# A table of decays in 32 rows with zeros below it, earlier products of zeros, and a second queue for the second batch's inputs

## Chip, cores, metric

One core of a Trainium2 chip (trn2). The metric is the device time of one execution in microseconds (us), as the median of several executions. A profile is one of these executions, recorded.

## The reference

```python
# recurrent attention: batch 4, heads 8, sequence 768, head size 64
for t in range(S):
    state = gamma * state + einsum('bhd,bhe->bhde', k[:, :, t], v[:, :, t])
    y[:, :, t] = scale * einsum('bhd,bhde->bhe', q[:, :, t], state)
# then, on x = y as (3072 tokens, 512):
h = x @ w_in                       # 512 -> 2048
out = maximum(0.01 * h, h) @ w_out # 2048 -> 512
```

## The kernel before

The attention is worked in chunks of 128 tokens. For each chunk and batch, `ap` is the product of k and q, `am` is `ap` under a mask, `yp` is the product of v (already multiplied by its decays) and `am`, and `x` is `yp` times the decays of q, the input of the two big products that fill nearly all of the time. The weights come as 64-bit numbers in pieces (`raw`), which ScalarE (ACT) and VectorE (DVE) turn into 32-bit ones (`w`); the first big product is called `d`.

The opening of the program is all that the change touches:

```python
rows = t[0:H, 1:3]...[:, 0 : decay.shape[1]]          # 8 rows of 780 numbers
nc.scalar.dma_start(out=rows, in_=decay)              # ScalarE's queue
load_qk(0, 0); load_v(0, 0)                           # SyncE's queue, in this order
load_qk(0, 1); load_v(0, 1)
load_piece(0); load_piece(1)
load_qk(0, 2); load_v(0, 2)
# ... [cut: further loads; memset of the mask by VectorE, its triangle by GpSimd]
nothing = t[:, 0, 0, :].bitcast(BF16)
nc.vector.memset(t[:, 0, 0, :], 0.0)                  # 256 columns of zeros
# keep_busy(n): n products of zeros, 512 columns each, into a spare bank
keep_busy(7)
score(0, 0)                                           # ap of batch 0
nc.tensor.matmul(tables[:, 0, 0:H], lhsT=by_head, rhs=ones, ...)          # decays of k
nc.tensor.matmul(tables[:, 0, H : H + HP], lhsT=place, rhs=g_c, ...)
masked(0, 0)                                          # am of batch 0, VectorE
nc.vector.tensor_copy(out=dec[:, n_gq:], in_=tables[:, 0, 0 : H + HP])
nc.tensor.matmul(spread..., lhsT=place, rhs=g_q, ...) # decays of q, 512 columns
nc.scalar.copy(out=dec[:, 0:n_gq], in_=spread...)
decay_v(0, 0, nc.vector)                              # v of batch 0 times its decays
score(0, 1); values(0, 0); masked(0, 1)               # values = yp
decay_v(0, 1)                                         # on GpSimd
keep_busy(1)
# ... [cut] taken(0, 0), values(0, 1), taken(0, 1): x of batches 0 and 1
score(0, 2)
keep_busy(3)
steps = direct(0, 0, x, parts[0][1], 0)               # d
# ... [cut]
```

Of the kernel before, what the change touches and what calls it, by code (L numbers as in the profile page):

```python
# [13 lines left out]
BF16 = mybir.dt.bfloat16  # L14
# [9 lines left out]
def kernel(  # L24
# [35 lines left out]
    nc = tc.nc  # L60
    NC = S // C
    DM = H * D
    HP = H // 2
# [11 lines left out]
    dec = const.tile([128, HP * C + H + HP], FP32, name="dec")  # L75
# [39 lines left out]
    heads = {}  # L115
# [11 lines left out]
            y = flat[:, half : 2 * half].rearrange("p (s h d) -> p s h d", s=2, h=H)  # L127
        heads[c, b] = x, y

    def load_qk(c, b):  # L130
        nc.sync.dma_start(out=heads[c, b][0], in_=qk[c, b])

    def load_v(c, b):
        nc.sync.dma_start(out=heads[c, b][1][:, 1], in_=kv[c, b][:, 1])

    def load_k(c, b):
        nc.sync.dma_start(out=heads[c, b][1][:, 0], in_=kv[c, b][:, 0])
# [1 line left out]
    def load(c, b, place=None):  # L139
        place_for(c, b, place)  # L140
        load_qk(c, b)
        nc.sync.dma_start(out=heads[c, b][1], in_=kv[c, b])

    def decay_v(c, b, engine=nc.gpsimd):
        v = heads[c, b][1][:, 1]
        if engine is not nc.scalar:
            engine.tensor_tensor(out=v, in0=v, in1=gk.unsqueeze(2).to_broadcast([128, H, D]),
                                 op=ALU.mult)
        else:
            for h in range(H):  # L150
                engine.activation(v[:, h], v[:, h], AF.Identity, scale=gk[:, h : h + 1])
# [6 lines left out]
    def score(c, b):  # L158

        x = heads[c, b][0]  # L160
        ps = scores[c, b] = two_banks(f"ap_{c}_{b}")
        for a in range(HP):
            for u in range(2):
                for j in range(2):
                    nc.tensor.matmul(ps[ts(u, 64), j, a, :], lhsT=x[ts(j, 64), 1, a, ts(u, 64)],  # L165
                                     rhs=x[ts(j, 64), 0, a, :])

    def masked(c, b):
        am = work.tile([128, 2, HP, C], FP32, tag="am", bufs=2, name=f"am_{c}_{b}")
        nc.vector.tensor_tensor(  # L170
            out=am.rearrange("p j a t -> p (j a) t"),
            in0=scores[c, b].rearrange("p j a t -> p (j a) t"),
            in1=mask.unsqueeze(1).to_broadcast([128, H, C]), op=ALU.mult)
        scores[c, b] = am
# [102 lines left out]
    def load_piece(n, place=None):  # L277
        if n >= N_PIECES:
            return
        if not f64:  # L280
            nc.sync.dma_start(out=piece(n), in_=weights[n].rearrange("p (h n) -> p h n", h=2))
            return
        if place is None:
            tag, bufs = ("raw", 3) if n < N_PIECES - 4 else (("qk", "kv")[n % 2], AHEAD)
            raws[n] = work.tile([128, W], I64, tag=tag, bufs=bufs, name=f"raw{n}")
        else:
            raws[n] = place.bitcast(I64)
        nc.sync.dma_start(out=raws[n], in_=weights[n])
# [299 lines left out]
    words = tile_x("words").rearrange("p i k n -> p (i k n)")[:, 0 : 2 * W]  # L588
    xs = {0: new_x(0)}
    x, t = xs[0]  # L590
    rows = t[0:H, 1:3].rearrange("p i k n -> p (i k n)")[:, 0 : decay.shape[1]]
    nc.scalar.dma_start(out=rows, in_=decay)
    load_qk(0, 0)
    load_v(0, 0)
    load_qk(0, 1)
    load_v(0, 1)
    load_piece(0)
    load_piece(1)
    load_qk(0, 2)
    load_v(0, 2)  # L600
    load_piece(2)
    load_piece(3, words)
# [14 lines left out]



    nothing = t[:, 0, 0, :].bitcast(BF16)  # L620
    nc.vector.memset(t[:, 0, 0, :], 0.0)
    idle = psum.tile([128, 2, N], FP32, tag="ff", bufs=4, name="idle")

    def keep_busy(n):
        for _ in range(n):
            nc.tensor.matmul(idle.rearrange("p i n -> p (i n)"), lhsT=nothing[:, 0:128],  # L626
                             rhs=nothing, start=True, stop=True, skip_group_check=True)



    tables = psum.tile([128, 2, N], FP32, tag="ff", bufs=4, name="tables")
    spread = psum.tile([128, 2, N], FP32, tag="ff", bufs=4, name="spread")
    n_gq = HP * C
    ends = [0, C, C + H, 2 * C + H, 2 * C + H + n_gq, 2 * C + H + n_gq + HP]
    by_head, ones, place, g_q, g_c = (rows[:, i:j] for i, j in zip(ends, ends[1:]))
    keep_busy(7)
    score(0, 0)
    nc.tensor.matmul(tables[:, 0, 0:H], lhsT=by_head, rhs=ones, start=True, stop=True,
                     skip_group_check=True)
    nc.tensor.matmul(tables[:, 0, H : H + HP], lhsT=place, rhs=g_c, start=False, stop=True,  # L640
                     skip_group_check=True)
    masked(0, 0)
    nc.vector.tensor_copy(out=dec[:, n_gq:], in_=tables[:, 0, 0 : H + HP])
    nc.tensor.matmul(spread.rearrange("p i n -> p (i n)"), lhsT=place, rhs=g_q, start=True,
                     stop=True, skip_group_check=True)
    nc.scalar.copy(out=dec[:, 0:n_gq], in_=spread.rearrange("p i n -> p (i n)"))
    decay_v(0, 0, nc.vector)
    score(0, 1)
    values(0, 0)
    masked(0, 1)  # L650
    decay_v(0, 1)
    keep_busy(1)
    next_powers()
    taken(0, 0, x)
    values(0, 1)
    next_mantissas(lambda: taken(0, 1, x))
    next_powers()
    score(0, 2)
    keep_busy(3)
    steps = direct(0, 0, x, parts[0][1], 0)  # L660
    next(steps)
# [121 lines left out]
def _decay(H, D):  # L783



    import numpy as np

    lg = np.log1p(-(2.0 ** (-5.0 - np.arange(H))))
    t = np.arange(1, C + 1)  # L790
    gq = np.exp(lg[:, None] * t[None, :]) / math.sqrt(D)
    gq = gq.reshape(H // 4, 2, 2, C).transpose(1, 2, 0, 3).reshape(2, -1)
    gc = np.exp(C * lg).reshape(H // 2, 2).T
    place = np.concatenate([np.repeat(np.eye(2), 64, axis=1), gq, gc], axis=1)
    place = np.concatenate([place, np.zeros((H - 2, place.shape[1]))])
    return np.concatenate([np.exp(-lg[:, None] * t[None, :]), np.eye(H), place],
                          axis=1).astype(np.float32)


def _layout(q, k, v, w_in, w_out):  # L800
# [60 lines left out]
```

## Time and profile before

| | before |
|---|---|
| median | 666.92 us of 3 runs (666.7 to 667.69); 666.81 of 6 with those beside the changed kernel |
| span of the profile | 664.9 us, of which TensorE busy 659.4 |
| first q and k land | 4.59 us |
| first `d` | 13.93 us |

The prediction below shows the views that it was read from. The columns used most: the chain of waits has start, length and what; the timeline has start, length, engine, line, operation, operands and, in brackets, the idle time before it and who ended it. The stretches: columns are the stretch, its length, busy time of PE, PEld (TensorE's loading of its left operand), DVE, ACT and POOL with the number of instructions, granted clock (the share of its full clock that TensorE was allowed), mean busy share of the 16 DMA engines, and GB/s. One caution: the trace's record of the clock begins when the full clock is first granted, and what lies before it is shown as 1.00, though the products there run at half rate. Before:

```profile
2.40:3.40 1.00, 1.00 (x4) 0.30 (x2) 0.00 (x0) 0.29 (x1) 0.00 (x0) 1.00 0.89 360
4.00:4.70 0.70, 0.63 (x6) 0.07 (x6) 0.00 (x0) 0.00 (x0) 0.00 (x0) 1.00 0.38 111
```

The DMA engines are busy and fast in the first stretch, and busy for a share of only 0.38 in the second.

### The profile page before, as it was taken

The numbers are of one execution on the slowest core, as the hardware profiler recorded it, in microseconds if no ns is written. First come the engines' busy times: TensorE is split into PE (matmuls) and PEld (weight loads), VectorE is DVE, ScalarE is ACT, GpSimd is POOL, SyncE is SP. The second block draws the span as 40 slices with busy tenths as digits, with TensorE's granted clock in tenths as the row PEclk, the third lists the DMA queues.
The fourth block names the chain that finished last, engine by engine and source line by source line (L and its number), as shares of the span: only waits on it lengthen the run. The fifth ranks groups of instructions, "written<-read, shape, count | busy, mean of one in ns | idle before, by whom it ended". The sixth has DMA issues, their size and how long they took to land.

```text
span 664.9 us, 10405 instructions
## 1 busy us (share of the span) xinstructions
PE 659.4 (99%) x4505; PEld 573.6 (86%) x4505; DVE 373.9 (56%) x570; ACT 175.8 (26%) x322; POOL 20.1 (3%) x22
## 2 busy tenths in 40 slices
PE   8999999999999999999999999999999999999998
PEld 5888888888888888888888888888888888888886
DVE  5789969889888676325543613663431444431342
ACT  5854555264261002212201311210221220221210
POOL 0000000000000111001000100100100000000000
PEclk9999999999999999999999999999999999999999
DMA  8920312313222453003012100301300001000001
GB/s 327 403 97 33 126 64 79 112 65 113 109 85 75 166 184 127 1 1 128 1 46 81 64 1 1 127 1 64 128 1 0 2 0 45 19 1 1 0 1 63
DMA packets 15758, 48.92 MB, mean 74 GB/s; under 512 B 1753, under 2 KB 2009, under 8 KB 15713
## 3 DMA queue, kind: packets, MB, share of 16 engines
q1 hardware_dynamic: 15696, 48.24, 20.1%
q8 instruction: 35, 0.57, 0.3%
q14 instruction: 11, 0.08, 0.0%
q10 hardware_dynamic: 16, 0.02, 0.0%
HBM read 41.97 MB, written 6.29 MB: 73 GB/s over the span
## 4 chain that ended last, share of the span: by engine, by line
PE 99%; DMA 1%; DVE 0%; issue 0%
PE B_o L414 13%; PE A_o L414 13%; PE C_o L414 12%; PE C_h L414 12%; PE B_h L414 12%; PE A_h L414 12%; PE D_o L414 6%; PE D_h L414 6%; PE ap L165 4%; PE yp L193 4%; PE d L436 2%; PE yp L184 2%; PE yp L208 1%; DMA qk<-in_qk_dram 1%; PE sums L208 0%; PE idle L626 0%
## 5 line engine op out<-in xcount | busy, mean ns | idle before, releaser
L414 PE MATMUL A_h<-x,w 128*128 128x256 f32 x368 | 87.0, 379 | 0.0
L414 PEld LDWEIGHTS A_h<-x,w 128*128 128x128 f32 x368 | 69.9, 190 | 9.6 <-issue 0.2
L414 PE MATMUL A_o<-g,w 128*128 128x256 f32 x288 | 68.0, 379 | 0.0
L449 ACT ACTIVATE g<-g 128x512 f32<-128x512 f32 x69 | 42.0, 630 | 92.4 <-DVE g L361 92.4
L414 PEld LDWEIGHTS A_o<-g,w 128*128 128x128 f32 x288 | 54.8, 190 | 7.4
L454 ACT COPY m<-A_h 128x512 f32<-128x512 f32 x23 | 13.4, 582 | 143.6 <-PE A_h L414 103.9
L361 DVE TENSOR_TENSOR m<-m,B_h 128x512 f32<-128x512 f32 x23 | 15.8, 686 | 55.5 <-PE B_h L414 55.5
L361 DVE TENSOR_TENSOR m<-m,B_o 128x512 f32<-128x512 f32 x16 | 11.0, 685 | 63.9 <-PE B_o L414 63.9
L238 DVE TENSOR_TENSOR x<-yp,dec 128x512 f32<-128x512 f32 x24 | 16.4, 689 | 49.7 <-PE yp L208 35.6
L414 PE MATMUL C_h<-t,w 128*128 128x256 f32 x184 | 44.1, 383 | 0.0
L414 PE MATMUL B_h<-x,w 128*128 128x256 f32 x184 | 44.1, 383 | 0.0
L414 PE MATMUL B_h<-t,w 128*128 128x256 f32 x184 | 43.5, 379 | 0.0
L414 PE MATMUL D_h<-t,w 128*128 128x256 f32 x184 | 43.5, 379 | 0.0
L414 PE MATMUL C_h<-x,w 128*128 128x256 f32 x184 | 43.5, 379 | 0.0
L414 PEld LDWEIGHTS C_h<-t,w 128*128 128x128 f32 x184 | 34.5, 190 | 5.5 <-issue 0.9
L414 PEld LDWEIGHTS B_h<-t,w 128*128 128x128 f32 x184 | 35.0, 190 | 4.7
L414 PEld LDWEIGHTS D_h<-t,w 128*128 128x128 f32 x184 | 35.0, 190 | 4.7
L414 PEld LDWEIGHTS C_h<-x,w 128*128 128x128 f32 x184 | 35.0, 190 | 4.7
L414 PEld LDWEIGHTS B_h<-x,w 128*128 128x128 f32 x184 | 34.5, 190 | 5.0 <-issue 0.3
L364 DVE TENSOR_TENSOR gd<-g,gd 128x512 f32<-128x512 f32 x48 | 37.1, 773 | 1.7
L170 DVE TENSOR_TENSOR am<-ap,mask 128x1024 f32<-128x1024 f32 x24 | 28.5, 1220 | 10.8 <-PE ap L165 10.8
L414 PE MATMUL B_o<-gd,w 128*128 128x256 f32 x144 | 34.0, 379 | 0.0
(118 smaller groups left out, 1019.0 us busy)
## 6 DMA issues: line engine op xcount, KB each, us to landing
raw<-in_weights_dram SPq DMA_DIRECT2D x31, 512.0 KB, 4.3
qk<-in_qk_dram SPq DMA_DIRECT2D x19, 512.0 KB, 3.8
kv<-in_kv_dram SPq DMA_DIRECT2D x17, 512.0 KB, 4.4
out_dram<-o SPq DMA_DIRECT2D x23, 256.0 KB, 2.1
in<-in_qk_dram SPq DMA_DIRECT2D x3, 512.0 KB, 8.7
in<-in_kv_dram SPq DMA_DIRECT2D x3, 512.0 KB, 8.5
kv<-in_kv_dram SPq DMA_DIRECT2D x4, 256.0 KB, 7.0
o_in<-in_qk_dram SPq DMA_DIRECT2D x2, 512.0 KB, 8.6
```

The costliest lines, as they stand in the source:

```text
L165: nc.tensor.matmul(ps[ts(u, 64), j, a, :], lhsT=x[ts(j, 64), 1, a, ts(u, 64)], rhs=x[ts(j, 64), 0, a, :])
L170: nc.vector.tensor_tensor(out=am.rearrange("p j a t -> p (j a) t"), in0=scores[c, b].rearrange("p j a t -> p (j a) t"), in1=mask.unsqueeze ...
L184: nc.tensor.matmul(ps[ts(i, 64), j, m, :], lhsT=st[b][ts(j, 64), a, :], rhs=x[ts(j, 64), 0, a, :], start=(m == 0), stop=False, skip_group_ ...
L193: nc.tensor.matmul(ps[ts(i, 64), j, m, :], lhsT=y[:, 1, 2 * a + j, :], rhs=am[:, j, a, :], start=(c == 0 and m == 0), stop=True, skip_grou ...
L208: nc.tensor.matmul(sp[ts(j, 64), a, :], lhsT=y[:, 0, 2 * a + j, :], rhs=y[:, 1, 2 * a + j, :], start=start, stop=True, skip_group_check=True)
L238: nc.vector.tensor_tensor(out=blocks, in0=ps[:, :, 0 : HP // 2, :], in1=gq, op=ALU.mult)
L361: nc.vector.tensor_tensor(out=out, in0=a, in1=b, op=ALU.add)
L364: nc.vector.tensor_tensor(out=out, in0=a, in1=b, op=ALU.subtract)
L414: nc.tensor.matmul(half, lhsT=block(w, sa)[:, k, ts(i, 128)], rhs=rhs[:, k, :], start=(first and (i == 0 or split) and n == 0 and k == 0), ...
L436: nc.tensor.matmul(banks[r][:, i, :], lhsT=block(2 * u, r + 2 * kh)[:, k, ts(i, 128)], rhs=x[:, 2 * kh + th, k, :], start=(step == 0 and i ...
L449: nc.scalar.activation(g[:, i], g[:, i], AF.Prelu, alpha=0.01)
L454: nc.scalar.copy(out=got["m1"], in_=ps)
```

## The change

The intent, as far as it can be read from the code: give the array zeros to multiply sooner and make the table products full ones of 128 rows, so that its clock comes up early; use ScalarE's queue for the second batch's loads so that the hole at 4 us is filled; and take two small jobs from VectorE.

```diff
+    def load_qk(c, b, queue=nc.sync):     # [cut: load_v in the same way]
-    rows = t[0:H, 1:3]...
-    nc.scalar.dma_start(out=rows, in_=decay)
+    rows = t[:, 1:3]...
+    n_rows = decay.shape[0]               # 32: 8 rows and 24 of zeros from memory
+    nc.scalar.dma_start(out=rows[0:n_rows], in_=decay)
+    nc.gpsimd.memset(rows[n_rows:64], 0.0)
+    nc.gpsimd.memset(rows[64:128], 0.0)
+    nothing = t[:, 0, 0, 0:64].bitcast(BF16)
+    nc.vector.memset(t[:, 0, 0, 0:64], 0.0)
-    load_qk(0, 1)
-    load_v(0, 1)
+    load_qk(0, 1, nc.scalar)
+    load_v(0, 1, nc.scalar)
@@ [cut: memset of the mask, now after that of the zeros]
-    keep_busy(7)
+    keep_busy(8)                          # 128 columns read four times over
@@
-    nc.vector.tensor_copy(out=dec[:, n_gq:], in_=tables[:, 0, 0 : H + HP])
+    nc.scalar.copy(out=dec[:, n_gq:], in_=tables[:, 0, 0 : H + HP])
-    decay_v(0, 0, nc.vector)
+    decay_v(0, 0)                         # GpSimd
```

More of the change, by code (lines that the diff above doesn't have):

```diff
@@ L128, in place_for, with load_v @@
         heads[c, b] = x, y
-    def load_qk(c, b):
-        nc.sync.dma_start(out=heads[c, b][0], in_=qk[c, b])
-    def load_v(c, b):
-        nc.sync.dma_start(out=heads[c, b][1][:, 1], in_=kv[c, b][:, 1])
+    def load_qk(c, b, queue=nc.sync):
+        queue.dma_start(out=heads[c, b][0], in_=qk[c, b])
+    def load_v(c, b, queue=nc.sync):
+        queue.dma_start(out=heads[c, b][1][:, 1], in_=kv[c, b][:, 1])
     def load_k(c, b):
@@ L590 @@
     x, t = xs[0]
-    rows = t[0:H, 1:3].rearrange("p i k n -> p (i k n)")[:, 0 : decay.shape[1]]
-    nc.scalar.dma_start(out=rows, in_=decay)
+    rows = t[:, 1:3].rearrange("p i k n -> p (i k n)")[:, 0 : decay.shape[1]]
+    n_rows = decay.shape[0]
[4 more added lines that the diff above has]
+    nc.vector.memset(t[:, 0, 0, 0:64], 0.0)
     load_qk(0, 0)
     load_v(0, 0)
-    load_qk(0, 1)
-    load_v(0, 1)
+    load_qk(0, 1, nc.scalar)
+    load_v(0, 1, nc.scalar)
     load_piece(0)
@@ L616 @@
     parts = [new_g(0, 0)]
-    nothing = t[:, 0, 0, :].bitcast(BF16)
-    nc.vector.memset(t[:, 0, 0, :], 0.0)
     idle = psum.tile([128, 2, N], FP32, tag="ff", bufs=4, name="idle")
@@ L625, in keep_busy @@
         for _ in range(n):
-            nc.tensor.matmul(idle.rearrange("p i n -> p (i n)"), lhsT=nothing[:, 0:128],
-                             rhs=nothing, start=True, stop=True, skip_group_check=True)
+            nc.tensor.matmul(idle.rearrange("p i (two n) -> p (i two) n", two=2), lhsT=nothing,
+                             rhs=nothing.unsqueeze(1).to_broadcast([128, 4, 128]),
+                             start=True, stop=True, skip_group_check=True)
     tables = psum.tile([128, 2, N], FP32, tag="ff", bufs=4, name="tables")
@@ L795, in _decay @@
     place = np.concatenate([place, np.zeros((H - 2, place.shape[1]))])
-    return np.concatenate([np.exp(-lg[:, None] * t[None, :]), np.eye(H), place],
-                          axis=1).astype(np.float32)
+    rows = np.concatenate([np.exp(-lg[:, None] * t[None, :]), np.eye(H), place], axis=1)
+    return np.concatenate([rows, np.zeros((32 - H, rows.shape[1]))]).astype(np.float32)
 def _layout(q, k, v, w_in, w_out):
```

## The prediction

> **What bounds the kernel now.** I read the page first, then the chain of waits of the first 30 us, then the timeline and the stretches of the first 14 us. On the page, the busy shares and the chain that ended last:
>
> ```profile
> PE 659.4 (99%) x4505; PEld 573.6 (86%) x4505; DVE 373.9 (56%) x570; ACT 175.8 (26%) x322; POOL 20.1 (3%) x22
> ...
> PE 99%; DMA 1%; DVE 0%; issue 0%
> ```
>
> TensorE (PE) is busy for 659.4 of the 664.9 us of the span, and 99% of the chain is its products. So there is little to win: 664.9 - 659.4 = 5.5 us are not product time, less than half of the 13.3 us that 2% of the time would be. The whole change lies in the first 14 us. The chain of waits of that stretch, each line start, length, what:
>
> ```profile
> 0.80 3.78 DMA qk<-in_qk_dram
> 4.59 0.04 issue
> 4.63 1.75 PE ap L165 x32
> 6.38 0.31 PE tables L638 x2
> 6.69 0.22 PE tables L640 x2
> 6.91 0.96 PE spread L644 x2
> 7.88 1.03 PE ap L165 x32
> 8.91 1.02 PE yp L193 x16
> ...
> 10.35 1.11 PE yp L193 x16
> 11.46 0.02 issue
> 11.48 0.70 DVE x L238
> 12.18 0.05 issue
> 12.23 1.10 PE ap L165 x32
> ```
>
> The first batch's q and k land at 4.59 us, and from then on TensorE's order sets the end. Two things stand out. The same 32 products of `ap` take 1.75 us the first time and 1.03 us the second. And the table products (0.31 + 0.22 + 0.96 = 1.49 us) stand in the chain. In the timeline, the products of zeros:
>
> ```profile
> 1.40 3.17 PE L626 MATMUL idle<-t 128*128 128x512 bf16 x7 [1.40 <-DVE t L621]
> ...
> 1.80 0.15 PEld L626 LDWEIGHTS <-t 128*128 128x128 bf16 x1 [0.28 <-issue]
> 2.23 0.15 PEld L626 LDWEIGHTS <-t 128*128 128x128 bf16 x1 [0.28 <-issue]
> 2.65 0.15 PEld L626 LDWEIGHTS <-t 128*128 128x128 bf16 x1 [0.28 <-issue]
> ```
>
> They start at 1.40, when VectorE (DVE) has cleared their operand, and follow each other by 0.43 us; the three of 13.27 to 13.93 follow each other by 0.22. So the array works at half rate at first. Inside the first `ap` the step per four products falls from 0.213 to 0.11 us at about 6.0: call that moment w, the time at which the array comes to full rate. From 12.23 us to 75 us I found no gap between products over 0.12 us beyond their own streaming, so a start earlier or later by d moves the end by d, as long as data are there.
>
> **What the Trainium skill says.** "TensorE: Matmul & The Clock Gate", Part 1: the array runs at half clock until it has been busy for a window of about 3.4 us, which runs free of the kernel, and successive 512-column products are then 427 ns apart, later 216 ns. The trace agrees on both steps (0.43 and 0.22 us) and on w: 6.0 - 1.4 = 4.6 us lies between one and two windows. No run here shows the window itself yet. The same page, LDWEIGHTS: a load costs by columns, not by contracted rows. The trace agrees: 188 ns for 8 rows of 128 columns, 190 ns for 128 rows. So 128 rows of table in place of 8 cost TensorE nothing. "DMA: Bandwidth & Descriptors", Queues, rings and completion order: SyncE and ScalarE each own a row of rings on the same 16 engines, and an engine takes turns between rows. Nothing in the kernel before shows two big loads on two queues at once. "SBUF — State Buffer", Who interferes with whom: a VectorE instruction with at most one SBUF input does not disturb GpSimd; `masked` reads PSUM and the mask, so the decay moved to GpSimd should not slow it.
>
> **The change part by part.**
>
> (1) Products of zeros sooner. Before: mask memset 0.17 us, then 256 columns 0.27 us, done at 1.34. After: first 64 columns. A line through 128 columns in 165 ns and 256 in 272 ns gives 112 ns for 64, so it is done at 0.90 + 0.11 = 1.01 and TensorE starts at about 1.06, 0.34 us earlier. Eight products at 0.427 end at 1.06 + 3.42 = 4.48, still under the landing at 4.59: the eighth costs nothing. Gain: w can come up to 0.34 us earlier. Work W measured at full rate, begun at S and half rate until w, ends at W + (S + w)/2. So 0.34 us of w is worth 0.17 us.
>
> (2) How w varies. With a free window, w lies anywhere between start + 3.4 and start + 6.8: 4.8 to 8.2 before. The profiled execution (w = 6.0) took 666.64; by the formula the others could take 666.64 - 0.6 to 666.64 + 1.1, and the timed ones took 666.7, 666.92 and 667.69. The two lower values stand close together; an early w would gain less, as the second batch's q and k land only at 7.59. I choose this as the reading of the spread. After: w in 4.5 to 7.9.
>
> (3) Second batch on ScalarE's queue. In the stretch 4.00 to 4.70 the DMA engines are busy for a share of 0.38 and move 111 GB/s, against 384 at 2.40 to 3.20 and 413 at 6.30 to 12.00: the third load of SyncE's queue, issued at 1.71, brings its first packet only at 4.68. A second queue would fill this hole; 0.7 us x (1 - 0.38) = 0.4 us of data come sooner. But nothing on the chain waits for them: q and k of batch 1 land at 7.59, and their products start at 7.81 because the table products end at 7.88. They are worth something only where w is early. Against it: ScalarE issues the table (0.80 to 1.38) and then q and k of batch 1 at about 1.4; from about 2.5 these share the 16 engines with batch 0's q and k, whose last packets run to about 4.2. If half of that stretch is lost, S rises from 4.63 to some 5.0 to 5.4. That costs (S - 4.63)/2 = 0.2 to 0.4 us where w comes later than S, and all of it where w is earlier.
>
> (4) Table as 32 rows, zeros below. Four times the bytes, 98 KB instead of 24: at 412 GB/s that is 0.24 us in place of 0.06 on the rings ahead of batch 1. GpSimd's two memsets of 780 columns I put at under 1 us each (its two-input product of 512 columns takes 1.07); they and the mask end by about 3.2, and are needed at 6.3. TensorE's time is unchanged, 1.49 us. The likely intent: products of 8 rows may not count as a busy array, and a window holding them may then not release the clock. In this trace w came before them, so it shows nothing; where w would fall at 7 or 8 this could save some tenths.
>
> (5) Copies. VectorE loses its copy (0.16) and decay (0.69). ScalarE copies the table right after the products (about 6.9 to 7.1), GpSimd takes the decay (1.07, done by about 8.3), and `yp` needs it at 8.84. VectorE was waiting at 8.56 to 8.98 anyway: 0 us.
>
> Sum: -0.17 (1), +0.2 to +0.4 (3), -0.0 to -0.5 for early landings and fuller rows (3, 4): between -0.5 and +0.3, centre about -0.3, with my view that such a change is written because an executed trace called for it.
>
> **The rivals.** (a) The first load becomes the bound: landing at 5.2 or later, TensorE idle after the eighth product of zeros, time 667.0 to 667.5. For it: rings taking turns and the hole filled; against: ScalarE's second issue comes 0.6 us after the first load's. (b) The clock is released a whole step sooner, by fuller products or by the earlier start falling into an earlier window: w near 4.5 to 5, time about 665.8 to 666.1. For it: w is worth half its shift, and the landing of batch 1 no longer stops it; against: by the page the window is free. (c) The transfer is hidden and nothing is seen: `ap` of batch 2 starts at 12.23 for VectorE's `x`, which ended at 12.18, and its own load landed at 12.10, so two things hold it within 0.1 us; time 666.9. (d) VectorE or ScalarE takes over later: both are over 0.9 busy from 14 to 20 us, but their chains start from the same products and would shift along.
>
> **Range and chances.** I predict 666.5 us, 0.4 under the median before. Range 665.7 to 667.4: w alone moves the time by over 1 us from execution to execution. 2% is 13.3 us, more than the whole start could give; slower by that much would need a stall no view hints at. Faster 0.01, same 0.98, slower 0.01.
>
> **What would show it.** First product of zeros at about 1.06 us (1). Landing of batch 0's q and k, 4.59 before: above 4.9 confirms the sharing, below 4.7 refutes it (3). The DMA share at 4.0 to 4.7 over 0.8 (3). Table products still 1.5 us in the chain (4). The second `ap` not waiting for its load, `yp` not waiting for GpSimd (5). The time to `ap` of batch 2 (12.23 before) minus the change of the end should be 0: if not, a stall later than 14 us was moved. The prediction would be wrong if w hardly varies, or if the load's loss exceeds 1 us.

## The result and the profile after

The changed kernel took 666.84 us (median of 6, 666.78 to 667.28); the kernel before 666.81 (median of 6, 666.53 to 667.69). The ratio is 1.0, with a 95% interval of 0.9987 to 1.0013. A ratio here is the mean time of one kernel's runs over the mean of the other's of the same rounds, so not quite the ratio of the medians.

The profiled execution of the changed kernel took 667.28 us, the longest of its six, so its profile shows a bad case; a second one follows in the experiments. The page:

```profile
PE 659.2 (99%) x4506; PEld 572.5 (86%) x4506; DVE 372.7 (56%) x568; ACT 175.9 (26%) x323; POOL 22.4 (3%) x25
...
PE 98%; DMA 1%; DVE 0%; POOL 0%; ACTq 0%; issue 0%; DVEq 0%
```

GpSimd (POOL) and ScalarE's sequencer (ACTq) have come into the chain. The timeline of TensorE, to be laid beside the zeros and `ap` of before:

```profile
1.06 3.27 PE L629 MATMUL idle<-t 128*128 128x512 bf16 x8 [1.06 <-DVE t L597]
5.58 1.10 PE L165 MATMUL ap<-qk 64*64 64x128 f32 x32 [1.24 <-DMA qk<-in_qk_dram]
```

The zeros start at 1.06 instead of 1.40, and `ap` runs at full rate from the start (1.10 us instead of 1.75). But q and k of batch 0 landed at 5.54 instead of 4.59, and TensorE stood idle for 1.24 us. The two stretches shown of before:

```profile
2.40:3.40 1.00, 1.00 (x4) 0.37 (x3) 0.00 (x0) 1.00 (x1) 0.29 (x1) 1.00 0.80 109
4.00:4.70 0.70, 0.34 (x2) 0.00 (x0) 0.00 (x0) 0.00 (x0) 0.00 (x0) 1.00 1.05 367
```

The hole at 4.00 to 4.70 is filled (367 GB/s instead of 111), but from 2.40 to 3.40 the engines are busy for a share of 0.80 and move only 109 GB/s. The chain of waits to the first `d`:

```profile
0.81 0.41 ACTq L593
...
1.73 8.20 DMA kv<-in_kv_dram
9.93 0.07 issue
10.00 1.05 POOL kv L147
11.05 0.04 issue
11.10 1.12 PE yp L193 x16
...
12.24 0.69 DVE x L238
12.93 0.61 DVE w L355
...
13.63 0.70 DVE w L357
14.33 0.04 issue
14.38 3.85 PE d L436 x16
```

It is another chain than before: v of batch 1, now on ScalarE's queue, lands only at 9.93, GpSimd multiplies it by its decays until 11.05, and TensorE waits for that; then VectorE's `x` and weights hold the first `d` until 14.38 (13.93 before).

### The profile page after: what moved, and what is told of

It reads as the page before. It is cut to its first block, busy times and chain, and to the rows that moved or that the text cites. A ratio compares the mean times of both kernels' runs of the same rounds, so it can differ in the third digit from the quotient of the medians.

```text
span 665.6 us, 10410 instructions
## 1 busy us (share of the span) xinstructions
PE 659.2 (99%) x4506; PEld 572.5 (86%) x4506; DVE 372.7 (56%) x568; ACT 175.9 (26%) x323; POOL 22.4 (3%) x25
## 4 chain that ended last, share of the span: by engine, by line
PE 98%; DMA 1%; DVE 0%; POOL 0%; ACTq 0%; issue 0%; DVEq 0%
PE B_o L414 13%; PE A_o L414 13%; PE C_o L414 12%; PE B_h L414 12%; PE C_h L414 12%; PE A_h L414 12%; PE D_o L414 6%; PE D_h L414 6%; PE yp L193 3%; PE ap L165 3%; PE d L436 2%; PE yp L184 2%; DMA kv<-in_kv_dram 1%; PE yp L208 1%; PE sums L208 0%; POOL kv L147 0%
## 5 line engine op out<-in xcount | busy, mean ns | idle before, releaser
L147 POOL TENSOR_TENSOR kv<-kv,dec 128x512 f32<-128x512 f32 x18 | 20.5, 1137 | 456.8 <-DMA kv<-in_kv_dram 440.8
```

Of the source, the lines that this page charges most:

```text
L147: engine.tensor_tensor(out=v, in0=v, in1=gk.unsqueeze(2).to_broadcast([128, H, D]), op=ALU.mult)
```

## The experiments

Twelve kernels, each on one chip with its own runs of the kernel before. All gave the right result. "Batch n lands" is the time of the last of the 16 semaphore updates (the signals by which the 16 DMA engines report their parts done) of its load of q and k; "full clock" is the moment from which the trace's clock record grants the whole clock.

The theory after reading the two traces: the table of 32 rows holds the DMA engines while the first load runs, and v of batch 1 is late because it is on the second queue. The rivals: the second queue's big load takes turns with the first one, as predicted; or the differences are only those of the clock's phase.

### Table and queue, two by two

`queue_back`, the changed kernel with batch 1 on SyncE's queue:

```diff
-    load_qk(0, 1, nc.scalar)
-    load_v(0, 1, nc.scalar)
+    load_qk(0, 1)
+    load_v(0, 1)
```

> The changed kernel with batch 1's q, k and v back on SyncE's queue; table of 32 rows and sooner zeros kept. Theory (the table of 32 rows holds the DMA engines from 2.4 to 3.4 us, 21 packets of 3120 B taking 300 to 770 ns): batch 0's q and k still land late, above 5.2 us (5.54 in the changed kernel, 4.59 before). Rival (the second big load on the other queue takes turns with the first): they land at 4.5 to 4.8. In both: batch 1's v lands at 8.0 to 8.9 instead of 9.93, GpSimd's decay of it no longer holds TensorE, first `d` before 14.0. Time: theory 666.4 to 666.9, rival 666.0 to 666.5.

Measured: 666.8 us (666.42, 666.45, 666.48, 667.12, and two at 669.96 and 670.36), before 667.0 (11 runs, two of them at 670.1); ratio 1.0006 [0.9978, 1.0034]. Batch 0 lands at 5.05, between the two expectations; v of batch 1 at 7.73. The `yp` of batch 1 starts at 10.18 and the first `d` at 13.45.

`table_of_8`, the changed kernel with the table of 8 rows and products of 8 rows:

```diff
-    rows = t[:, 1:3]...
-    nc.scalar.dma_start(out=rows[0:n_rows], in_=decay)
-    nc.gpsimd.memset(rows[n_rows:64], 0.0)
-    nc.gpsimd.memset(rows[64:128], 0.0)
+    rows = t[0:H, 1:3]...
+    nc.scalar.dma_start(out=rows, in_=decay)
```

> The changed kernel with the table of 8 rows as before, products of 8 rows, no zeros by GpSimd; batch 1 stays on ScalarE's queue. Theory (table): batch 0's q and k land at 4.5 to 4.9 us. Rival (two queues taking turns): they stay above 5.2. In both, batch 1's v still lands late, 9 us or later, because its 2 KB packets take turns with the 4 KB packets of the weights. Time: theory 666.3 to 666.8 (v of batch 1 keeps holding `yp`), rival 666.8.

Measured: 666.99 (666.48 to 667.75), ratio 0.999 [0.9972, 1.0009]. Batch 0 lands at 4.72, as the theory said; v of batch 1 at 9.09. The profile shows something not expected. The stretches:

```profile
4.00:7.30 3.30, 2.90 (x41) 1.61 (x39) 1.22 (x1) 0.17 (x1) 0.61 (x1) 1.00 1.02 376
7.40:10.70 3.30, 3.30 (x46) 2.97 (x48) 1.23 (x1) 2.41 (x4) 1.38 (x2) 0.50 1.03 414
10.80:20.00 9.20, 8.80 (x111) 6.37 (x111) 8.06 (x13) 9.01 (x25) 0.00 (x0) 1.00 1.04 401
```

The granted clock was 1.00 from 3.95 us, fell to 0.50 at 7.37 and came back at 10.78. Both steps are 3.41 us apart. The first window holds 0.4 us of idleness and the products of 8 rows. In the changed kernel, with a full clock from 3.88, the same window holds more idleness (1.24 us) and products of 128 rows, and the clock stayed.

`zeros_only_q`, both undone, the sooner zeros and the moved copies kept:

> Both undone: table of 8 rows and batch 1 on SyncE's queue; products of zeros sooner (8, from 64 columns) and the copies on other engines kept. Start of the zeros at 1.06, batch 0 lands at 4.6, batch 1's v at 8.3. Theory: the sooner zeros are worth half the shift of the moment at which the array comes to full rate, so 666.4 to 666.7 by median, 0.1 to 0.4 below the kernel before in the same rounds, and the profile shows full rate between 3.8 and 7.9 us. Rival (the sooner zeros bring nothing, as a load holds the array anyway): within 0.1 of the kernel before.

Measured: 666.93 (666.73 to 667.92) against 667.0, ratio 0.9993 [0.9974, 1.0012]. Batch 0 lands at 4.54, v of batch 1 at 8.01, full clock at 5.55. The gain of 0.1 to 0.4 is not seen: 0.07, within the noise. Its second `ap` started at 7.56 instead of 7.81, but the `ap` of batch 2 at 12.19 instead of 12.23: it waited for its load, which landed at 12.06 (12.10 before). From the chain of waits:

```profile
4.01 8.05 DMA o_in<-in_qk_dram
12.06 0.14 issue
12.19 1.10 PE ap L165 x32
```

What follows. Batch 0 lands at 5.54 (both changes), 5.05 (table alone), 4.72 (queue alone), 4.54 (neither). That is one execution each, and the changed kernel profiled again (`after_again`, below) landed at 5.01, so such differences are uncertain by half a microsecond. All profiles of this document together are clearer: with the table of 32 rows issued first, batch 0 lands at 4.99 to 5.54 in five profiles with batch 1's q and k on ScalarE's queue and at 5.05 to 5.55 in three with them on SyncE's; with the table of 8 rows issued first, at 4.54 to 4.72 in three. The table of 32 rows delays the first load; an effect of the queue on it is not seen.

The time that the table's packets took fits this in direction, not in size. In the trace of the changed kernel the 32 packets of 3120 bytes took 404 ns each in the mean, two on each of the 16 engines: 32 x 404 / 16 = 0.81 us per engine; the 8 of `table_of_8` took 449 ns, 0.22 us. That is 0.59 more, and batch 0 landed 0.82 later. In `queue_back` against `zeros_only_q` it is 0.54 - 0.18 = 0.36 more, and 0.51 later. And batch 1's q and k did not take turns with batch 0's: on ScalarE's queue their first packet started at 4.79 in the changed kernel, when the last of batch 0's did (4.85).

### Table later

`table_late` is `zeros_only_q` with ScalarE loading its function table (a dummy copy) before it issues the table of 8 rows:

```diff
-    nc.scalar.dma_start(out=rows, in_=decay)
     nc.vector.memset(t[:, 0, 0, 0:64], 0.0)
+    nc.scalar.copy(out=early, in_=t[:, 0, 0, 0:1])     # [cut: the tile early]
+    nc.scalar.dma_start(out=rows, in_=decay)
```

> As the one with both undone, but ScalarE loads its function table first and issues the decay table (8 rows) after that, about 2.4 us, so that its packets stand behind those of batch 0's q and k. Theory (the table's packets at the head delay the first load): batch 0 lands 0.1 to 0.5 us sooner than 4.59, the table before 6 us, and the time falls to 666.1 to 666.5. Rival (the start of the rings themselves is slow, whatever comes first): landing 4.5 to 4.7 and the time equal to the one with both undone.

Measured: 667.16 (666.24 to 669.79), ratio 0.9998 [0.9976, 1.0019]. A miss: batch 0 lands at 4.80, not sooner. (The issue stands at 1.03 in the trace, not at 2.4, but the table's packets started only at 3.49.) The rival comes nearer. The table's packets took 124 ns each there, against 332 at the head of the queues in the kernel before: the packet is slow because it is among the first, not because of its size. Why the first ones are slow stays open.

`table32_late` does the same with the table of 32 rows and `queue_back`'s loads:

> Batch 1 on SyncE's queue, table of 32 rows, but issued by ScalarE after its function table, at about 2.2 us instead of 0.81. Theory (at the head of the queues the table's packets are slow, 270 to 400 ns on average, and hold the first load; later they take 125 ns, as the 8-row table issued late showed): batch 0's q and k land at 4.6 to 4.9 instead of 5.05, the table before 5.3, and the time is 0 to 0.2 us under that with the table at the head, 666.3 to 666.6. Rival (later loads pay what the first saves): landing of batch 1's v later by as much, time unchanged.

Measured: 666.81 (666.66 to 666.95), ratio 0.9996 [0.9983, 1.0009]. A miss again: batch 0 lands at 5.16, and v of batch 1 at 8.36, 0.63 later than in `queue_back`, as the rival said. The packets ran from 3.46 to 4.82, that is beside the last packets of batch 0 instead of its first.

### What a product of 8 rows does to the clock

To make the suspicion of `table_of_8` independent of the window's phase, the product `spread` was made 20 times, over 128 rows or over 8, with the same loads and result:

```diff
+    for _ in range(20):
         nc.tensor.matmul(spread..., lhsT=place, rhs=g_q, ...)   # or place[0:H], g_q[0:H]
```

> The changed kernel with its product of the decays over 128 rows (512 columns, 0.43 us at full rate) made 20 times in place of once, same result. 19 x 0.427 = 8.1 us more of it, so that at least one whole clock window of 3.41 us holds nothing else. Theory (products of 128 rows, zeros or not, keep the array at full clock; products of 8 rows do not): granted clock 1.0 throughout, the 20 products 0.427 us apart, time 673.5 to 675. Rival (rows do not matter for the clock): the same as the one with 8 rows.

> The same, but the 20 products take only the first 8 rows of the table (same loads, same result). Theory: the clock record shows half rate for at least one window of 3.41 us after the 8-row products have filled a window, and the time is 1.5 to 5 us above the one with 128 rows. Rival (rows do not matter): granted clock and time equal to the one with 128 rows, within 0.5 us.

Measured: 683.13 with 128 rows (682.75 to 683.45), 700.06 with 8 (699.54 to 701.13). The 128-row one is higher than expected because such a product makes two passes (x40 in the trace), so 19 more take 19 x 0.854 = 16.2 us; that was an error of the expectation. The 8-row one is 16.9 us above it instead of 1.5 to 5, as the clock did not come back while those products ran. The stretches, first 128 rows, then 8:

```profile
6.50:9.80 3.30, 3.30 (x11) 1.63 (x12) 1.16 (x1) 0.17 (x1) 1.39 (x2) 1.00 1.04 412
9.90:23.90 14.00, 14.00 (x34) 5.96 (x32) 0.00 (x0) 0.00 (x0) 0.60 (x1) 1.00 1.03 400
```

```profile
9.90:43.90 34.00, 34.00 (x88) 14.54 (x88) 1.87 (x3) 4.42 (x9) 0.61 (x1) 0.50 0.43 166
44.00:60.00 16.00, 15.60 (x214) 12.47 (x211) 12.64 (x19) 10.00 (x31) 0.00 (x0) 1.00 0.64 231
```

With 8 rows TensorE is busy for all 34.00 us of the stretch, and the granted clock is 0.50 throughout; it falls at 9.86 and comes back at 43.99, ten windows of 3.41 us. The products of 8 rows fill the first 29.4 us of the stretch (to 39.32); `ap` and `yp` follow, and with them the clock comes back. With 128 rows, 120 of them zeros, it stays at 1.00. This settles what the 32-row table is good for: products of 8 rows did not keep the array's clock up, products of 128 rows did, though 120 of the rows were zeros.

The record shows the same without a profile. Each run lists its mean granted clock. One window at half rate after the full clock costs 3.41 / 2 of some 665 us and so shows as 0.997; the profiled execution of `table_of_8` (667.75 us) has it. A first full clock that is merely late does not show: `tables_first_2`, below, has 1.0. Of the kernels with products of 8 rows (before, `table_of_8`, `zeros_only_q`, `table_late`), 9 of the 49 runs with a clock on record have 0.997 or less, with times of 667.6 to 669.8; of those with products of 128 rows, none of 47.

### v of batch 1, and the changed kernel again

`after_again` is the changed kernel, unaltered:

> The changed kernel once more, unaltered, as the control of this call and for a second profile. Theory (the loads set the start): batch 0's q and k land at 5.2 to 5.8, batch 1's v at 9.2 to 10, whatever the moment of full clock; the third `d` step starts at 19.8 to 20.3; median 666.7 to 667.0. Rival (the first profile was an unusual execution): batch 0 at 4.6 to 5.0 or batch 1's v before 9.

Measured: 666.92 (666.85 to 667.11), ratio 1.0001 [0.9988, 1.0013]. Batch 0 landed at 5.01, a little below the expectation, v of batch 1 at 9.30, and the clock was full only at 6.38. So the first profile was an extreme, not another kind: its table packets took 404 ns, here 247 (32 x 247 / 16 = 0.49).

`v1_on_sync`, with only v of batch 1 back on SyncE's queue:

```diff
-    load_v(0, 1, nc.scalar)
+    load_v(0, 1)
```

> The changed kernel with only batch 1's v back on SyncE's queue; its q and k stay on ScalarE's. Theory (v of batch 1 is late because its 2 KB packets take turns one for one with 4 KB packets of the weights): v of batch 1 lands at 7.5 to 8.6 instead of 9.93, GpSimd no longer holds `yp`, `yp` of batch 1 starts before 10.7 (11.10), time 0.2 to 0.5 under the changed kernel of the same call. Rival (the whole stream is late): v above 9, time as the changed kernel.

Measured: 666.44 (666.28 to 666.84), ratio to the kernel before 0.9995 [0.9982, 1.0007]. All five runs lie under all five of `after_again` on the same chip: means 666.55 and 666.95. v lands at 7.66. GpSimd in `after_again` and then in `v1_on_sync`, from the timeline:

```profile
7.61 1.04 POOL L147 TENSOR_TENSOR kv<-kv,dec 128x512 f32<-128x512 f32 x1 [4.90 <-ACT dec L648]
9.37 1.04 POOL L147 TENSOR_TENSOR kv<-kv,dec 128x512 f32<-128x512 f32 x1 [0.72 <-DMA kv<-in_kv_dram]
```

```profile
7.53 2.05 POOL L147 TENSOR_TENSOR kv<-kv,dec 128x512 f32<-128x512 f32 x2 [4.82 <-ACT dec L648]
```

The wait for the load is gone. (Its profiled execution, 666.84, was its slowest, with the clock full at 6.23; there VectorE's `am` held `yp` until 10.67, so v was not what it waited for. Nor was it in `after_again`, where GpSimd was done at 10.41 and `yp` started at 10.76: the 0.08 us between these two profiles are what the moments of full clock give. I read the quicker ones as executions with an earlier clock, which the late v would have stopped; they were not profiled.) Why v is late on ScalarE's queue is seen in the DMA queues of the changed kernel from 7.0 to 8.5 us (queue 1 is SyncE's, 10 is ScalarE's; packets, MB, share):

```profile
q1 hardware_dynamic: 105, 0.39, 65.1%
q10 hardware_dynamic: 111, 0.22, 37.6%
```

The two queues move one packet each in turn, semaphore writes included. But v's packets have 2048 bytes and those of the weights 4096, so v gets about a third of the bytes, and its 256 KB take as long as 768 KB would. That rests on these counts: the packet size was not varied, and on SyncE's queue v also stands ahead of the weights instead of beside them.

### The suspected cost doubled

`table_of_64`, 64 rows of table from memory:

```diff
-    nc.gpsimd.memset(rows[n_rows:64], 0.0)
-    ... np.zeros((32 - H, ...))
+    ... np.zeros((64 - H, ...))
```

> The suspected cost doubled: the changed kernel with a table of 64 rows sent from memory instead of 32 (64 packets of 3120 B, 4 on each DMA engine), GpSimd's zeros in the upper half only. Theory (each packet of the table at the head costs the engine 270 to 400 ns, or at least its 125 ns later on): batch 0's q and k land 0.25 to 0.8 us later than in the changed kernel, at 5.8 to 6.3; time 0.1 to 0.5 above it. Rival (the delay is a fixed cost of the second queue's start): landing as in the changed kernel, 5.2 to 5.6.

Measured: 668.2 (668.16 to 668.5), ratio 1.0021 [1.0007, 1.0035]. Slower than expected, and for another reason: batch 0 landed at 4.56. The table's packets moved only from 3.35 to 4.66, after most of batch 0's, and held what came behind them on ScalarE's queue: v of batch 1 landed at 10.50, q and k of batch 1 at 8.55. (The full clock, too, came late, at 7.02, but `yp` waited for v until 11.67.) So a larger table is not simply a longer delay of the first load; what counts is when its packets come. Why they came later stays open.

### Small products first

`tables_first` tries to beat both: batch 1 on SyncE's queue, the two small table products while TensorE waits for q and k, one product of zeros before `d` instead of three.

```diff
     keep_busy(8)
+    nc.tensor.matmul(tables[:, 0, 0:H], ...); nc.tensor.matmul(tables[:, 0, H : H + HP], ...)
     score(0, 0)
-    nc.tensor.matmul(tables[:, 0, 0:H], ...); nc.tensor.matmul(tables[:, 0, H : H + HP], ...)
...
-    keep_busy(3)
+    keep_busy(1)
```

> An attempt to beat both: batch 1 on SyncE's queue, and the two small table products stand before batch 0's products, while TensorE waits for q and k anyway; one product of zeros instead of three before the first `d`. By the profile with batch 1 back on SyncE's queue: the table lands at 4.42, q and k at 5.05, so the 0.44 us of small products leave the chain; second `ap` from 7.63 to 7.2, first `d` from 13.45 to about 12.9. Time 665.8 to 666.3. Rival (VectorE's chain of weights sets the first `d`): gain under 0.2 us.

Measured: 666.46 (665.85, 666.16, 666.18, 666.73, 668.17, 668.4), ratio 0.9997 [0.9983, 1.001]; first `d` at 13.21. The fastest executions, and two slow ones. Hence the repetition, `tables_first_2`:

> The attempt with the small table products first and batch 1 on SyncE's queue, repeated beside the changed kernel. Theory: fast executions at 665.8 to 666.3, 0.5 to 0.9 under the changed kernel's median in the same rounds, with some executions near 668.4 as before; third `d` step before 19.2. Rival (the first result was luck of the clock): median within 0.2 of the changed kernel.

Measured: 668.3 (666.33, and four from 668.25 to 668.63), ratio 1.0016 [1.0004, 1.0029]. No improvement, then. The profile shows why. TensorE:

```profile
5.10 0.57 PE L642 MATMUL tables<-t 128*128 128x8 f32 x2 [0.44 <-DMA t<-decay_dram]
5.52 0.57 PE L644 MATMUL tables<-t 128*128 128x4 f32 x2
6.01 1.99 PE L165 MATMUL ap<-qk 64*64 64x128 f32 x32
7.93 2.01 PE L649 MATMUL spread<-t 128*128 128x512 f32 x2
```

Everything runs at half rate: the clock was full only at 9.75. By my reading, waits at both ends of the small products, and products of 8 and 4 columns, left the window from 2.93 to 6.34 too empty; no run tests it. A full clock one window later costs 3.41 / 2 = 1.7 us, most of the 2 us between the two groups of times. The executions near 670 of the kernel before and of `queue_back` lie two such steps above the rest, at a mean clock of 1.0; that fits a late full clock, but none of them was profiled. Those of the kernel before near 668 (0.997) are the fallen clock of above.

### What the profiles say together

Times in us of the profiled execution; `yp` is that of batch 1, batch 2 is its q and k, d3 the third step of `d`.

| kernel | full clock | batch 0 lands | 2nd `ap` | v of batch 1 | `yp` | batch 2 lands | d3 | time |
|---|---|---|---|---|---|---|---|---|
| before | 6.01 | 4.59 | 7.81 | 8.25 | 10.35 | 12.10 | 19.53 | 666.64 |
| changed | 3.88 | 5.54 | 8.12 | 9.93 | 11.10 | 12.01 | 20.22 | 667.28 |
| after_again | 6.38 | 5.01 | 8.21 | 9.30 | 10.76 | 11.55 | 19.87 | 666.92 |
| queue_back | 4.91 | 5.05 | 7.63 | 7.73 | 10.18 | 11.58 | 19.29 | 666.42 |
| zeros_only_q | 5.55 | 4.54 | 7.56 | 8.01 | 10.10 | 12.06 | 19.49 | 666.73 |
| table32_late | 3.81 | 5.16 | 7.74 | 8.36 | 10.28 | 12.21 | 19.65 | 666.76 |
| v1_on_sync | 6.23 | 4.99 | 8.13 | 7.66 | 10.67 | 11.51 | 19.79 | 666.84 |
| tables_first_2 | 9.75 | 5.55 | 9.87 | 8.18 | 12.41 | 12.03 | 21.53 | 668.63 |

From d3 to the end of the span it is 645.32 to 645.36 us in all twelve experiments and both kernels: whatever happens, happens before 20 us. And d3 follows from two times: it is the later of `yp` + 9.12 and batch 2's landing + 7.43. That meets all eight rows within 0.02 us (before: 19.47 and 19.53, measured 19.53; changed: 20.22 and 19.44, measured 20.22). I fitted the two constants to these traces. Five others meet the rule within 0.01 us: `table_of_8` (20.41, measured 20.42), `table_late` (19.93, 19.93), `table_of_64` (20.79, 20.79), `tables_first` (19.06, 19.05) and `spread20_128rows` (35.70, 35.69); `spread20_8rows` is off by 0.17, as its `yp` began 0.38 us before the full clock. In all six `yp` decides, so the second constant rests on three rows of the table alone. As I read them, the first constant is VectorE's chain of `x` and weights with the products behind it, the second the `ap` of batch 2, the zeros and the products. So before, the load of batch 2 set the end, and `yp` stood 0.06 us behind it. In the changed kernel that load comes sooner by 0.1 to 0.55, and `yp` is later by 0.4 to 0.75.

## Why the prediction was right or wrong

The time was foreseen within its range (666.5 predicted, 666.84 measured, range 665.7 to 667.4), and "same" with it. Its steps did less well, and the number does not come from them: the parts add up to between -0.47 and +0.23, centre -0.12, which is 666.8 from the median of 666.92. The centre of -0.3, and the last step down to 666.5, came from the view that such a change is written because a trace called for it. Measured against its own six runs of before, the change is +0.03 us. That the bare sum would have met this is luck, as its terms were wrong in ways that cancel.

- **The bound, and where the change acts**: right. TensorE's 99% and the constant 645.3 us after d3 show it.
- **(1) Sooner zeros**: start at 1.06 as worked out. The formula W + (S + w)/2 holds where w is later than S, with S the start of the first `ap`: between before and `after_again` S rises from 4.63 to 5.05 and w from 6.01 to 6.38, which makes 0.40; the second `ap` moved from 7.81 to 8.21. The step that failed is that this gain is passed on: `zeros_only_q` was 0.25 ahead at the second `ap` (part of it may be where its window fell) and 0.04 at d3, as the load of batch 2 landed as before. The prediction had that under rival (c), "two things hold it within 0.1 us", and gave it no share in the sum.
- **(2) How w varies**: the free window is right, with its 3.41 us steps. The bounds were not: 2.8 us after the start (3.88) and 8.7 (9.75) both occurred. A window need not be busy from end to end, and it may fail. Counting back 3.41 us from the full clock gives the window that released it: zeros in 2.75 us of it were enough in `table32_late` (1.06 to 3.81), 2.54 us were not in `table_of_64` (1.06 to 3.60; full clock at 7.02). In these profiles, then, w lies from about 2.7 to 6 us after the start of the zeros, not 3.4 to 6.8, and later only in `tables_first_2`, where a further window failed.
- **(3) Second queue**: "from about 2.5 these share the 16 engines with batch 0's q and k" failed. They did not meet: ScalarE's first packet of batch 1 started at 4.79, batch 0's last at 4.85. The landing at 5.54 passed the test set for it, "above 4.9 confirms the sharing", and the test was too weak: another cause gave the same number. What the queue really does, delaying v of batch 1 by 1.1 to 2.2 us in the three pairs that differ in it (9.09 against 8.01, 9.30 against 7.66, 9.93 against 7.73), was not in the working. The hole at 4.0 to 4.7 was filled as foreseen.
- **(4) Table**: the mis-sized term. "0.24 us in place of 0.06 on the rings ahead of batch 1" was worked out at 412 GB/s; measured it is 0.5 to 0.8 us per engine in the two profiles of the changed kernel, and beside batch 0's load. The guess about 8-row products was right, and `spread20_8rows` shows it; in the sum it had only a part of "-0.0 to -0.5", and it acts in another way than was supposed there: in the profiled executions they made a full clock fall again (`table_of_8` at 7.37), where the prediction thought of a first full clock that comes late. GpSimd's memsets took 0.74 each, done in time, and the table products 1.50 in the chain of `after_again`, as foreseen.
- **(5) Copies**: cost nothing, as said (GpSimd's decay took 1.04 us beside VectorE's `am`, 1.07 before); but "`yp` not waiting for GpSimd" failed in the first profile through the late v.
- **The check on the end**: "the time to `ap` of batch 2 minus the change of the end should be 0" failed: it began at 12.14 instead of 12.23 while d3 was 0.69 later. `d` waited for VectorE, which rival (d) had held to shift along. (It also read VectorE as over 0.9 busy from 14 to 20 us; the stretch has 5.30 of 6.00, 0.88.)
- **Rivals (a) and (b)**: the profiled execution looks like (a): landing at 5.54, TensorE idle for 1.24 us after the eighth product of zeros, 667.28 in a range of 667.0 to 667.5. But not for its reason, two loads taking turns, and v of batch 1 was the later wait. It had (b)'s early clock as well, at 3.88, and not (b)'s time of 665.8 to 666.1.

In sum, two gains (a clock that does not fall back, and a filled hole) met two losses (first load by 0.4 to 0.95, v by 1.1 to 1.7), and the sizes cancel. That the clock no longer falls back shows in the clock on record: 9 of 49 runs with products of 8 rows, none of 47 with 128 rows. The spread of the times shows less than it seems to: 666.78 to 667.28 over the eleven runs of the changed kernel, 666.26 to 670.13 over the 37 of before beside all of them, the first three included; but `queue_back`, with the same table, reached 670.36. That the late v narrows the spread from below is not shown. `v1_on_sync` undoes one of the losses and has the lowest median of all, 0.06% under the changed kernel beside it; against the kernel before that is not clear of noise.

## What to carry to other kernels

Where a program starts, list what lands when, and put a number on each packet size in each queue before moving a load to a second queue: the queues take turns by packet, so the load with small packets loses (by the packet counts of one stretch; sizes were not varied). Keep the array's clock up with products over all 128 rows; products of 8 did not count here, however busy TensorE looked. And look at the mean clock of every run, not only at the profiled one: it told fallen clocks from late ones. And when a test for a cause is written down, choose one that the rival causes would fail.

## What the Trainium skill lacked or had wrong

- "TensorE: Matmul & The Clock Gate", Part 1, says that the clock follows how busy the array has been; of what counts as busy, the page only says (Part 4) that transposes do not count in the same way, and nothing of rows. Here products of 8 rows held TensorE busy for 29.4 us without a break at a granted clock of 0.50; products of 128 rows, 120 of them zeros, kept 1.00.
- The same part gives the full clock after about 3.4 us of sustained work, in a free-running window. The window is confirmed (steps of 3.41 us); a full clock came already 2.8 us after the first product (1.06 to 3.88), with a window filled for 2.75 us (`table32_late`) but not with one filled for 2.54 (`table_of_64`), and a window with 1.24 us of idleness at a stretch kept it.
- "DMA: Bandwidth & Descriptors", Issuing engines are not separate DMA queues, says that issuing from several engines saves only the sequencer's time. The queue also settles who comes first: v of batch 1 landed at 9.09 to 10.50 on ScalarE's queue (six profiles) and 7.66 to 8.56 on SyncE's (eight). The taking of turns by packet (Queues, rings and completion order) agrees: 105 and 111 packets, 0.39 and 0.22 MB in 1.5 us.
- No page has the cost of the first packets of a program: packets of 3120 bytes took 247 to 404 ns in the mean at 2 to 4 us (32 rows at the head, changed kernel), and 124 ns once the first load was under way (8 rows, `table_late`).
